# Four small products moved apart on TensorE, and one unit of the inverse transform placed a quad earlier

## The chip, the core and the metric

The program runs on one core of a Trainium2 chip. The time is the device time of that core in microseconds, as a median of several executions. The engines that work side by side are TensorE (PE in the profile, with PEld for its weight loads), VectorE (DVE), ScalarE (ACT), GpSimd (POOL) and the queues that start DMA transfers (SP). A `L407` in a profile line is a line of the kernel's source, in the numbering of the kernel before the change.

## What is computed

A filter in the frequency domain along the sequence, and then a two-layer network with an ELU between the layers:

```python
batch, seq, dim = (8, 3008, 256)
X = np.fft.rfft(x, axis=1)
F = (filt_r + 1j * filt_i)[None, :, :]
y = np.fft.irfft(X * F, n=x.shape[1], axis=1)
# 24064 tokens of 256, hidden width 2048
h = y.reshape(B * S, D) @ w_in
g = np.where(h > 0.0, h, alpha * (np.exp(np.minimum(h, 0.0)) - 1.0))
out = g @ w_out
```

## The kernel before

The transform of length 3008 = 47 x 64 is done as products with small tables. For each batch there is a first factor forward (`a_unit`), a second one with the filter behind it (`b_unit`, eight units `g` of four frequencies `k2` each), the step back through the second factor (`bi_unit`, which takes two units `g` at a time and is called the double step back), and the third factor (`n_unit`, six units `m`), whose output is the input of the network. The network does the two large products by a scheme of seven products in place of eight, so each of its inputs comes with sums and differences of its four blocks (`combine`).

One *item* of the network is a batch, a part `m` of six, and a quarter `q` of the hidden width. An item is called a *quad*, and a batch has 24 of them. While the network works on batch `b - 1`, the transform of batch `b` is put between its steps, by a plan that says in which quad (numbered 0 to 23 within a batch below), and whether in the middle (`place` 0) or at the end (`place` 1), a unit stands.

The double step back, with 16 products of 24 rows and 32 columns, each on its own 32 x 32 piece of the TensorE array. `a` chooses the piece's rows and the PSUM bank, `p` its columns. In the first one of a batch (`g == 0`) the frequency `k2 = 0` needs a table of its own (`v = 1`) for half of the columns when `a = 0`; so there these four products are split in two halves (`js`), and the count is 20:

```python
    def bi_unit(b, g):
        z = ss.pop((b, g))
        t = t3s[b, g] = t3p.tile([P, 2, 4, D], FP32, tag="t3", name="t3")
        pv = [bank("pv") for _ in range(4)]
        for p in range(4):
            for a, (_, ps) in enumerate(pv):
                for js, v in ((slice(0, 1), 1), (slice(1, 2), 0)) if g == a == 0 else ((slice(0, 2), 0),):
                    r = slice(32 * a, 32 * a + 24)
                    nc.tensor.matmul(ps[32 * p:32 * p + 32, js, :], bb[r, v, p, :], z[r, p, js, :],
                                     start=True, stop=True, tile_position=(32 * a, 32 * p))      # L407
        for a, (i, ps) in enumerate(pv):
            nc.scalar.activation(out=t[:, :, a, :], in_=ps, func=AXT.Copy)                       # L410
            banks.append(i)
```

`bank()` hands out four PSUM banks in turn; a matmul into a bank waits until its last reader is done. The third factor, and the sums:

```python
    def n_unit(b, m):
        t, w, h = t4s.pop((b, m)), tns.pop((b, m)), half(m)
        rows = []
        for dh in range(2):
            y = yp.tile([P, 512], FP32, tag="y%d" % dh, name="y%d" % dh)
            k, ps = bank("psn", (P, 512))
            for q, i in enumerate(order(m)):
                nc.tensor.matmul(ps[:, ts(q, P)], ...)                                          # L441
            nc.scalar.activation(out=y[:, 0:2 * h], in_=ps[:, 0:2 * h], func=AXT.Copy)          # L443
            banks.append(k)
            rows += [y[:, 0:h], y[:, h:2 * h]]
        s = yp.tile([P, 3, 256], FP32, tag="ys", name="ys")
        ys[b, m] = combine(*rows, *(s[:, i, 0:h] for i in range(3)))

    def combine(b11, b12, b21, b22, t1, t2, t4):
        nc.vector.tensor_tensor(out=t1, in0=b12, in1=b11, op=ALU.subtract)      # L464
        nc.vector.tensor_tensor(out=b12, in0=b22, in1=b12, op=ALU.subtract)     # L465
        nc.vector.tensor_tensor(out=t2, in0=b22, in1=t1, op=ALU.subtract)       # L466
        nc.vector.tensor_tensor(out=t4, in0=b21, in1=t2, op=ALU.subtract)       # L467
        ...
```

The steps of an item up to the hidden layer (`U`), cut to what the text speaks of. Step `s4` adds onto the bank that step `s7` filled, so its matmul (phd L489) must wait until VectorE has read that bank for `b22` (L497):

```python
        def mm(n, key, start): ...                                   # L489, bank "ph" + key
        def add(o, i0, i1): nc.vector.tensor_tensor(...)             # L497
        def s2(): add("b11", mm(2, "a", True), g["t1"]); done("a")
        ...
        def s7(): add("b22", mm(7, "d", True), g["t4"]); elu_max("b11", g["b11"])
        def s3(): ...
        def s4(): add("b21", mm(4, "d", False), g["t2"]); done("d"); elu_max("b22", g["b22"])
```

The steps down (`D`, L571) multiply with `w_out`; after the last quad of a part, `c_unit` makes four more sums of its result on VectorE (L587). The plan, and the order of the steps in a quad:

```python
                for g in range(NG):
                    s = t + 9 + g + g // 2
                    at(s, 1, b_unit, b, g)          # quads 9 10 12 13 15 16 18 19, at the end
                    ...
                    if g % 2:
                        opens.add(s + 2)
                        at(s + 1, 1, bi_unit, b, g - 1)     # quads 11 14 17 20, at the end
                        at(s + 1, 1, y_write, b, g - 1)
            for m, (s, place) in enumerate(((23, 0), (25, 1), (29, 1), (32, 0), (36, 0), (41, 0))):
                if b > 0 or m > 0:
                    at(t + s - 2, 0, tn_read, b, m)
                    at(t + s - 2, 0, y_read, b, m)
                    at(t + s, place, n_unit, b, m)          # m = 5: quad 41 - 24 = 17, in the middle
                at(t + PER + 4 * m + 5, 0, c_unit, b, m)    # quads 5 9 13 17 21 1, in the middle
                at(t + PER + 4 * m + 6, 0, o_unit, b, m)
        ...
            for k in "DUUDUDDU" if i in opens else "UUDUDDU": ...
            for fn, a in plan.get((i, 0), ()): fn(*a)
            for k in "DUUDUD" if i in opens else "DUUDUDD": ...
            if up_tail: up_tail()
            if down_tail: down_tail()
            for fn, a in plan.get((i, 1), ()): fn(*a)
```

Of the kernel before, what the change touches and what calls it, by code (L numbers as in the profile page):

```python
# [122 lines left out]
def order(m):  # L123

    return (1, 2, 3, 0) if m == 0 else tuple(range(4 * m, 4 * m + 4))
# [3 lines left out]
def kernel(  # L129
# [9 lines left out]
    nc = tc.nc  # L139
# [6 lines left out]
    def pool(name, bufs, **kw):  # L146
        return ctx.enter_context(tc.tile_pool(name=name, bufs=bufs, **kw))
# [21 lines left out]
    bb = pairs[:, P:3 * P].rearrange("p (v a i) -> p v a i", v=2, a=4)  # L169
# [8 lines left out]
    xs, tas, tns, t1s, t2s, ss, t3s, t4s, zs, yds, ys, g_of, po_of, cs_, sds = ({} for _ in range(15))  # L178
# [8 lines left out]
    def bank(name, shape=(P, 2, D)):  # L187
        i = banks.pop(0)
        return i, psM.tile(list(shape), FP32, tag="m%d" % i, name=name)
# [209 lines left out]
    def bi_unit(b, g):  # L399
        z = ss.pop((b, g))  # L400
        t = t3s[b, g] = t3p.tile([P, 2, 4, D], FP32, tag="t3", name="t3")
        pv = [bank("pv") for _ in range(4)]
        for p in range(4):
            for a, (_, ps) in enumerate(pv):
                for js, v in ((slice(0, 1), 1), (slice(1, 2), 0)) if g == a == 0 else ((slice(0, 2), 0),):
                    r = slice(32 * a, 32 * a + 24)
                    nc.tensor.matmul(ps[32 * p:32 * p + 32, js, :], bb[r, v, p, :], z[r, p, js, :],  # L407
                                     start=True, stop=True, tile_position=(32 * a, 32 * p))
        for a, (i, ps) in enumerate(pv):
            nc.scalar.activation(out=t[:, :, a, :], in_=ps, func=AXT.Copy)  # L410
            banks.append(i)
# [18 lines left out]
    def half(m):  # L430

        return 224 if m == 0 else 256
# [8 lines that stand above are left out]
                nc.tensor.matmul(ps[:, ts(q, P)], t[:, i - 4 * m, ds(dh * P, P)], w[:, i - 4 * m, :],  # L441
                                 start=True, stop=True)
            nc.scalar.activation(out=y[:, 0:2 * h], in_=ps[:, 0:2 * h], func=AXT.Copy)  # L443
            banks.append(k)
            rows += [y[:, 0:h], y[:, h:2 * h]]
        s = yp.tile([P, 3, 256], FP32, tag="ys", name="ys")
        ys[b, m] = combine(*rows, *(s[:, i, 0:h] for i in range(3)))

# [11 lines left out]
# [6 lines that stand above are left out]
        return {1: b11, 2: b21, 3: b22, 4: t4, 5: t1, 6: t2, 7: b12}  # L468
# [207 lines left out]
    def w_join(k):  # L676
        q, j = divmod(k, 4)
        m, e, f, l = wts.pop(k)
        hi = wds.pop(k)[:, :, 1]
        nc.vector.scalar_tensor_tensor(out=e, in0=hi, scalar=0x80000000, in1=e,  # L680
                                       op0=ALU.bitwise_and, op1=ALU.bitwise_or)
        nc.vector.tensor_tensor(out=f, in0=f, in1=l, op=ALU.add)
        e = e.bitcast(FP32)
        if j < 2:
            f, e = (t.rearrange("p (a j c) -> p a j c", a=2, j=2) for t in (f, e))
            dst = w_in[q][:, 2 * j:2 * j + 2, :, :].rearrange("p j a c -> p a j c")
            nc.vector.tensor_tensor(out=dst, in0=f, in1=e, op=ALU.mult)
        else:

            f, e = (t.rearrange("p (i a e s) -> p i e a s", i=2, a=4, e=2) for t in (f, e))  # L690
            dst = w_out[q][:, 0:4, j - 2, :].rearrange("p (i e) (a s) -> p i e a s", i=2, a=4)
            for i in range(2):
                nc.vector.tensor_tensor(out=dst[:, i], in0=f[:, i], in1=e[:, i], op=ALU.mult)
        if j % 2 == 1 and k < 15:
            w_sums(k)

    def w_sums(k):
        q, j = divmod(k, 4)
        w = (w_in if j < 2 else w_out)[q]
        a11, a21, a12, a22, s1, s2, s4 = (w[:, i] for i in range(7))  # L700
        nc.vector.tensor_tensor(out=s1, in0=a21, in1=a22, op=ALU.add)
        nc.vector.tensor_tensor(out=s2, in0=s1, in1=a11, op=ALU.subtract)
        nc.vector.tensor_tensor(out=s4, in0=a12, in1=s2, op=ALU.subtract)
        nc.vector.tensor_tensor(out=a21, in0=a11, in1=a21, op=ALU.subtract)
# [30 lines left out]
    with tc.manual_schedule():  # L735
# [108 lines left out]
        ep = pool("ep", 2)  # L844
        op = pool("op", 1)
        n_unit(0, 0)
        w_join(14)


# [4 lines left out]
        def at(quad, place, fn, *a):  # L854
            plan.setdefault((quad, place), []).append((fn, a))
# [13 lines left out]
        for b in range(B):  # L869
            t = (b - 1) * PER  # L870
            if b > 0:
                for c, s in enumerate((2, 2, 4, 4, 7, 7)):
                    at(t + s, 0, x_unit, b, c)
                    if c % 2 == 0:
                        opens.add(t + s + 1)
                        at(t + s, 1, a_unit, b, c)
                    nb, nxt = (b, c + XBUFS) if c + XBUFS < NXC else (b + 1, c + XBUFS - NXC)
                    if nb < B:
                        at(t + s, 1, x_load, nb, nxt)
                    at(t + s, 1, z_write, b, c)  # L880
                for g in range(NG):
                    s = t + 9 + g + g // 2
                    at(s, 1, b_unit, b, g)
                    at(s - 2, 1, f_read, b, g)
                    at(s - 2, 1, z_read, b, g)
                    if g % 2:

                        opens.add(s + 2)
                        at(s + 1, 1, bi_unit, b, g - 1)
                        at(s + 1, 1, y_write, b, g - 1)  # L890
            for m, (s, place) in enumerate(((23, 0), (25, 1), (29, 1), (32, 0), (36, 0), (41, 0))):
                if b > 0 or m > 0:
                    at(t + s - 2, 0, tn_read, b, m)
                    at(t + s - 2, 0, y_read, b, m)
                    at(t + s, place, n_unit, b, m)
                at(t + PER + 4 * m + 5, 0, c_unit, b, m)
                at(t + PER + 4 * m + 6, 0, o_unit, b, m)

        items = [(b, m, q) for b in range(B) for m in range(6) for q in range(4)]
        for i in range(-PER, len(items) + 3):  # L900
# [3 lines left out]
            for k in "DUUDUDDU" if i in opens else "UUDUDDU":  # L904
                s = ups if k == "U" else downs
# [4 lines left out]
            for k in "DUUDUD" if i in opens else "DUUDUDD":  # L910
                s = ups if k == "U" else downs
# [40 lines left out]
```

## Time and profile before

| | |
|---|---|
| time, median of 3 executions | 2637.86 us (2635.85 to 2638.11) |
| the execution that was profiled | 2634.84 us, span 2632.7 us |
| PE busy (matmuls) | 2580.3 us, 98% |
| PEld busy (weight loads) | 2220.9 us, 84% |
| DVE busy | 1861.9 us, 71% |
| ACT busy | 1505.4 us, 57% |
| POOL busy | 488.8 us, 19% |
| mean granted TensorE clock | 0.995 |

The span starts with about 100 us for the first batch's transform and the weights; after that the network runs in a pattern of some 318.5 us for each batch until the end. A float32 matmul stands as two records in the trace. A busy share of 98% for PE does not say that the array streams data for 98% of the time: [...]records of different 32 x 32 pieces lie over each other.

### The profile page before, as it was taken

What the parts mean: (1) busy time and instruction counts of PE and PEld (TensorE: products, weight loads), DVE (VectorE), ACT (ScalarE), POOL (GpSimd) and SP (SyncE); (2) the same over time, 40 slices, a digit from 0 to 9 for tenths busy, and PEclk for the clock granted to TensorE, in tenths of its full rate; (3) what the DMA queues carried; (4) which work ended last, traced back from release to release, by engine and by line L of the source; (5) the groups of instructions that cost most, each with busy time, mean ns of one, the idle gap of its engine ahead of it and who ended that gap; (6) DMA issues with size and microseconds to landing.
All of it is one profiled execution on the core that took longest, in us unless ns stands there. A gap on an engine that the chain in (4) does not pass through costs nothing.

```text
span 2632.7 us, 41233 instructions
## 1 busy us (share of the span) xinstructions
PE 2580.3 (98%) x15300; PEld 2220.9 (84%) x15300; DVE 1861.9 (71%) x3203; ACT 1505.4 (57%) x2622; POOL 488.8 (19%) x669
## 2 busy tenths in 40 slices
PE   6799999999999999999999999999999999999998
PEld 4688889887898888988889888898889888898887
DVE  6876776677666776777667767677676668766666
ACT  7665555555565555555555555555555555555554
POOL 5102320024100331004300133002330023200000
PEclk9899999999999999999999999999999999999999
DMA  9544222432224232333314331143321332210010
GB/s 296 166 119 101 63 64 56 120 77 70 67 59 115 63 92 48 82 89 81 77 45 104 83 95 47 45 110 95 86 57 43 87 85 63 63 41 20 21 28 16
DMA packets 228840, 206.51 MB, mean 78 GB/s; under 512 B 130962, under 2 KB 194674, under 8 KB 228640
## 3 DMA queue, kind: packets, MB, share of 16 engines
q1 hardware_dynamic: 211328, 166.90, 25.7%
q0 software_dynamic: 15856, 36.25, 4.9%
q8 instruction: 121, 1.98, 0.3%
q10 hardware_dynamic: 1456, 0.72, 0.1%
q14 instruction: 79, 0.65, 0.1%
HBM read 131.91 MB, written 78.17 MB: 80 GB/s over the span
## 4 chain that ended last, share of the span: by engine, by line
PE 95%; DVE 1%; ACT 1%; DMA 0%; issue 0%; DVEq 0%; SPq 0%; ACTq 0%
PE po L571 43%; PE phs L489 25%; PE phd L489 12%; PE pha L489 6%; PE psn L441 3%; PE psr L376 2%; PE psa L228 2%; PE pv L407 1%; DVE ys L464 0%; PE po L324 0%; DMA yd<-t 0%; DVE ys L466 0%; PE psi L376 0%; ACT e L507 0%; DVE g L497 0%
## 5 line engine op out<-in xcount | busy, mean ns | idle before, releaser
L571 PE MATMUL po<-g,wo 128*128 128x256 f32 (+1 forms) x5376 | 1305.4, 376 | 0.0
L571 PEld LDWEIGHTS po<-g,wo 128*128 128x128 f32 x5376 | 1014.4, 190 | 143.8 <-issue 23.0
L500 ACT ACTIVATE g<-phs 128x512 f32<-128x512 f32 (+1 forms) x576 | 339.2, 589 | 823.1 <-PE phs L489 823.1
L497 DVE TENSOR_TENSOR g<-phd,g 128x512 f32<-128x512 f32 (+1 forms) x384 | 259.4, 676 | 402.5 <-ACT e L507 345.5
L507 ACT ACTIVATE e<-e 128x512 f32<-128x512 f32 (+1 forms) x768 | 477.3, 621 | 24.4
L511 DVE SCALAR_TENSOR_TENSOR g<-e,g 128x512 f32<-128x512 f32 (+1 forms) x576 | 397.2, 690 | 1.6 <-ACT e L507 1.3
L489 PE MATMUL phs<-y,wi 128*128 128x256 f32 (+1 forms) x1536 | 394.2, 379 | 0.0
L489 PE MATMUL phs<-ys,wi 128*128 128x256 f32 (+1 forms) x1536 | 387.7, 375 | 1.5 <-ACT g L500 1.5
L506 ACT ACTIVATE e<-g 128x512 f32<-128x512 f32 (+1 forms) x576 | 353.2, 613 | 42.8 <-DVE g L497 25.5
L489 PEld LDWEIGHTS phs<-y,wi 128*128 128x128 f32 x1536 | 284.4, 190 | 55.5 <-issue 11.5
L489 PEld LDWEIGHTS phs<-ys,wi 128*128 128x128 f32 x1536 | 291.4, 190 | 35.4 <-ACT g L500 2.5
L385 POOL TENSOR_TENSOR sr<-sr,zs 128x512 f32<-128x512 f32 x56 | 71.2, 1271 | 1144.5 <-DVE zs L330 1144.5
L511 DVE SCALAR_TENSOR_TENSOR g<-e,phs 128x512 f32<-128x512 f32 (+1 forms) x192 | 129.8, 676 | 126.6 <-ACT e L507 126.6
L489 PE MATMUL phd<-ys,wi 128*128 128x256 f32 (+1 forms) x768 | 195.2, 377 | 7.0 <-DVE g L497 7.0
L506 ACT ACTIVATE e<-phs 128x512 f32<-128x512 f32 (+1 forms) x192 | 113.0, 589 | 148.8 <-PE phs L489 148.7
L489 PE MATMUL phd<-y,wi 128*128 128x256 f32 (+1 forms) x768 | 193.7, 375 | 0.0
L489 PE MATMUL pha<-y,wi 128*128 128x256 f32 (+1 forms) x768 | 193.7, 375 | 0.0
L489 PEld LDWEIGHTS phd<-ys,wi 128*128 128x128 f32 x768 | 144.6, 190 | 28.6 <-DVE g L497 12.8
L497 DVE TENSOR_TENSOR g<-pha,g 128x512 f32<-128x512 f32 (+1 forms) x192 | 129.1, 672 | 53.3 <-PE pha L489 53.0
L489 PEld LDWEIGHTS pha<-y,wi 128*128 128x128 f32 x768 | 145.8, 190 | 16.5
L489 PEld LDWEIGHTS phd<-y,wi 128*128 128x128 f32 x768 | 145.8, 190 | 16.5
L548 DVE TENSOR_TENSOR g<-g,g 128x512 f32<-128x512 f32 (+1 forms) x192 | 130.7, 681 | 6.7
(129 smaller groups left out, 2382.5 us busy)
## 6 DMA issues: line engine op xcount, KB each, us to landing
yd<-t SPq DMA_DIRECT2D x127, 192.0 KB
t<-yd SPq DMA_DIRECT2D x190, 128.0 KB
z<-t SPq DMA_DIRECT2D x84, 256.0 KB
f<-fp POOLq DMA_DIRECT2D x224, 96.0 KB, 3.1
t<-z SPq DMA_DIRECT2D x224, 96.0 KB
out_dram<-o SPq DMA_DIRECT2D x632, 32.0 KB
tn<-tn_t SPq DMA_DIRECT2D x48, 256.0 KB
xc<-in_x_dram SPq DMA_DIRECT2D x84, 128.0 KB
```

What stands on the lines that cost most here:

```text
L228: nc.tensor.matmul(p[o:o + 64, u, :], w[r, u, o:o + 64], src[r, u, :], start=True, stop=True)
L376: nc.tensor.matmul(ps[32 * a:32 * a + 32, c, :], fb[k, 1 if g == a == 0 else 0, c, :], t[k, a, :], start=True, stop=True)
L385: nc.gpsimd.tensor_tensor(out=sr, in0=sr, in1=p, op=ALU.add)
L441: nc.tensor.matmul(ps[:, ts(q, P)], t[:, i - 4 * m, ds(dh * P, P)], w[:, i - 4 * m, :], start=True, stop=True)
L489: nc.tensor.matmul(ps[:, a, 0:h], w_in[q][:, COMBO[n], a, :], y[n], start=start and a == 0, stop=True, skip_group_check=True)
L497: nc.vector.tensor_tensor(out=g[o], in0=i0, in1=i1, op=ALU.add)
L500: nc.scalar.activation(out=g[o], in_=i0, func=AXT.Copy)
L506: nc.scalar.activation(out=e, in_=src, func=AXT.Relu, scale=-1.0)
L507: nc.scalar.activation(out=e, in_=e, func=AXT.Exp, scale=-1.0)
L511: nc.vector.scalar_tensor_tensor(out=g[n], in0=es[n], scalar=1.0, in1=src, op0=ALU.subtract, op1=ALU.max)
L548: nc.vector.tensor_tensor(out=b12, in0=b22, in1=b12, op=ALU.subtract)
L571: nc.tensor.matmul(po[i][:, u, 0:h], w_out[q][:, COMBO[n], a, :], g[n][:, a, :], start=q == 0 and a == 0 and n in (1, 3, 6, 4), stop=True, ...
```

## The change

There are two changes that have nothing to do with each other.

In the first double step back of a batch, the order of the 20 products is another: first the four with the table for `k2 = 0`, then the twelve whole ones of `a = 1, 2, 3`, then the four remaining halves of `a = 0`. Before, the two halves on one piece of the array stood next to each other. The products, their tables and their results are the same; for `g > 0` nothing changes.

The third factor's last unit (`m = 5`) goes from the middle of quad 17 to the middle of quad 16, and its reads from quad 15 to quad 14; its four sums on VectorE are put into a function of their own, which stands at the end of quad 17, behind the double step back of that quad. For all other `m` the sums stay where they were. The aim is to keep the four sums out of the middle of quad 17, where VectorE has products of `b_unit` and the four sums of `c_unit` as well.

```diff
-        for p in range(4):
-            for a, (_, ps) in enumerate(pv):
-                for js, v in ((slice(0, 1), 1), (slice(1, 2), 0)) if g == a == 0 else ((slice(0, 2), 0),):
-                    r = slice(32 * a, 32 * a + 24)
-                    nc.tensor.matmul(ps[32 * p:32 * p + 32, js, :], bb[r, v, p, :], z[r, p, js, :],
-                                     start=True, stop=True, tile_position=(32 * a, 32 * p))
+
+        both = [(p, a, slice(1 if g == a == 0 else 0, 2), 0) for p in range(4) for a in range(4)]
+        if g == 0:
+            both = [(p, 0, slice(0, 1), 1) for p in range(4)] + [w for w in both if w[1]] + [w for w in both if not w[1]]
+        for p, a, js, v in both:
+            r = slice(32 * a, 32 * a + 24)
+            nc.tensor.matmul(pv[a][1][32 * p:32 * p + 32, js, :], bb[r, v, p, :], z[r, p, js, :],
+                             start=True, stop=True, tile_position=(32 * a, 32 * p))
 ...
-        ys[b, m] = combine(*rows, *(s[:, i, 0:h] for i in range(3)))
+        ys[b, m] = rows + [s[:, i, 0:h] for i in range(3)]
+
+    def n_sums(b, m):
+        ys[b, m] = combine(*ys[b, m])
 ...
         n_unit(0, 0)
+        n_sums(0, 0)
 ...
-            for m, (s, place) in enumerate(((23, 0), (25, 1), (29, 1), (32, 0), (36, 0), (41, 0))):
+            for m, (s, place) in enumerate(((23, 0), (25, 1), (29, 1), (32, 0), (36, 0), (40, 0))):
                 if b > 0 or m > 0:
                     at(t + s - 2, 0, tn_read, b, m)
                     at(t + s - 2, 0, y_read, b, m)
                     at(t + s, place, n_unit, b, m)
+
+                    at(*((t + s + 1, 1) if m == 5 else (t + s, place)), n_sums, b, m)
```

## The prediction

> **What bounds the kernel now.** I read the page's busy shares and its chain of work first, then the waits of TensorE, then the two places that the change touches.
>
> ```profile
> PE 2580.3 (98%) x15300; PEld 2220.9 (84%) x15300; DVE 1861.9 (71%) x3203; ACT 1505.4 (57%) x2622; POOL 488.8 (19%) x669
> ...
> PE 95%; DVE 1%; ACT 1%; DMA 0%; issue 0%; DVEq 0%; SPq 0%; ACTq 0%
> ```
>
> TensorE is busy nearly always, and the chain that ended last lies on it for 95%. So time is won only where TensorE waits, or where its instructions run badly, and what is won there shortens the whole kernel as long as no other engine takes over; VectorE at 71% and ScalarE at 57% leave room on average. The waits of TensorE between 200 us and 2600 us, that is in the repeating pattern, are a single row (in total, times, longest):
>
> ```profile
> PE phd L489 <- DVE g L497: 7.0, 7, 1.0
> ```
>
> Seven times a matmul of step `s4` waits for VectorE. One of them is at 969 us, in quad 17 of a batch. The timeline there, first TensorE, then VectorE (start, duration, engine, line, what, idle before it):
>
> ```profile
> 967.15 1.03 PE L571 MATMUL po<-g,wo 128*128 128x256 f32 x4
> 969.17 1.13 PE L489 MATMUL phd<-ys,wi 128*128 128x256 f32 x4 [0.99 <-DVE g L497]
> ...
> 964.30 0.61 DVE L587 TENSOR_TENSOR c<-k,k 128x256 f32<-128x256 f32 x1
> 965.27 1.05 DVE L464 TENSOR_TENSOR ys<-y 128x256 f32<-128x256 f32 x1 [0.36 <-ACT y L443]
> 966.43 0.76 DVE L465 TENSOR_TENSOR y<-y,y 128x256 f32<-128x256 f32 x1
> 967.11 0.94 DVE L466 TENSOR_TENSOR ys<-y,ys 128x256 f32<-128x256 f32 x1
> 968.09 0.43 DVE L467 TENSOR_TENSOR ys<-y,ys 128x256 f32<-128x256 f32 x1
> 968.43 0.68 DVE L497 TENSOR_TENSOR g<-phd,g 128x512 f32<-128x512 f32 x1
> ```
>
> The reader is to see that the add L497, for which the matmul waits, stands directly behind the four sums of the third factor, and these behind a sum of `c_unit`. A group of four matmul records runs on from one start to the next in 0.86 us where nothing holds it (939.62 to 940.48 us in quad 15); here it is 969.17 - 967.15 = 2.02 us, so the loss is 1.16 us: 0.99 us of idle time[...]. All seven lie between 1.15 and 1.17 us. For quad 13, which has products of `b_unit` and a `c_unit` but no third factor, the same place reads:
>
> ```profile
> 911.81 1.03 PE L571 MATMUL po<-g,wo 128*128 128x256 f32 x4
> 912.83 1.13 PE L489 MATMUL phd<-ys,wi 128*128 128x256 f32 x4
> ```
>
> 1.02 us, so 0.16 us is lost there. Then the double step back, in the first one of a batch (g = 0, 40 records) and in the next one (g = 2, 32 records), each with the TensorE instruction that follows it:
>
> ```profile
> 248.86 2.14 PE L407 MATMUL pv<-zs,pairs 24*32 24x256 f32 x40
> 250.93 0.92 PE L571 MATMUL po<-g,wo 128*128 128x256 f32 x3
> ...
> 291.88 1.14 PE L407 MATMUL pv<-zs,pairs 24*32 24x512 f32 x32
> 292.95 0.92 PE L571 MATMUL po<-g,wo 128*128 128x256 f32 x3
> ```
>
> From its start to the next instruction the first takes 2.07 us, the other 1.07 us, though both stream the same number of columns. Why, is seen in the groups of matmuls in flight from 248.85 to 248.99 us, then from 248.99 to 249.25 us, and for g = 2 from 291.85 to 291.99 us:
>
> ```profile
> L407 PE MATMUL pv<-zs,pairs 24*32 24x512 f32 x9 | 0.7, 612 | 0.0
> L407 PE MATMUL pv<-zs,pairs 24*32 24x256 f32 x4 | 0.5, 398 | 0.0
> ...
> L407 PE MATMUL pv<-zs,pairs 24*32 24x256 f32 x8 | 0.7, 386 | 0.0
> L407 PE MATMUL pv<-zs,pairs 24*32 24x512 f32 x9 | 0.7, 612 | 0.0
> ...
> L407 PE MATMUL pv<-zs,pairs 24*32 24x512 f32 x16 | 0.7, 612 | 0.0
> ```
>
> Nine of the twelve whole products start within 0.14 us, and the four first halves; then no further whole one for over 0.25 us. The missing three are the last in program order (p = 3). With g = 2 all sixteen start at once.
>
> [...]nine whole products started while second halves before them in the order still waited. [...]the sums L464 to L467 take 0.42 us at the median and 1.05, 0.76 and 0.94 us in quad 17, where GpSimd adds at the same time; the fourth, after it was done, took 0.43 us.
>
> **The change part by part. First, the order of the products.** It removes no instruction: 20 products, 40 loads and 40 matmul records, seven times in the run (batches 1 to 7). Before, the second half on a piece follows the first in the order[...]. In the new order the four first halves and the twelve whole products [...]start at once, as in g = 2. [...]Their chain on one piece, from the single records of before, is: first pass at 0, second pass 0.24 us later, then the other half's passes 0.22 us apart, at 0.46 and 0.67 us, and 0.37 us for the last one's record: 1.05 us, and 0.04 us more for the fourth piece, 1.09 us. The whole products need 1.14 us, as in g = 2. So the halves lie beside them, and I put the start of the next instruction at 1.10 us, 0.03 us above g = 2 for the later issue. Gain 2.07 - 1.10 = 0.97 us, times 7: 6.8 us. Behind it ScalarE empties the bank of a = 0 first, which is now filled last, at about 1.09 us; in g = 2 it is also filled near the end, and the copies began there 1.3 us after the start of the products. So I expect the copies at the same distance and no new wait beyond the 0.1 us that g = 2 shows.
>
> **Second, the sums.** Without the third factor in its middle, quad 17 becomes what quad 13 is now: products, c sums, then L497. The four sums with their gaps hold VectorE from 965.27 to 968.43 us, 3.16 us; TensorE loses 1.16 us of that, and should lose 0.16 us as in quad 13. Gain 1.00 us, times 7: 7.0 us. The eighth batch's last unit has no transform beside it and no wait now, so nothing is won there.
>
> Third, what is added elsewhere. The 16 matmul records of the third factor (1.78 us) move from quad 17 to quad 16, nothing gained or lost. In quad 16 ScalarE gets its two copies (1.07 us) before the two copies L576 (1.07 us): before, it was through with L507 at 951.45 us and its next need, the copy for L506, was at 952.31 us; with both pairs it ends about 953.6 us, and TensorE, itself 1.75 us later there, asks at about 954.05 us. No wait. At the end of quad 17 VectorE gets four sums of 0.42 us, 1.7 us; it idled 0.99 us there before L497 reads pha (976.01 us), so that add comes about 0.7 us later. What needs it is ScalarE's L506 some 4 us later and a bank that comes round later still. No wait.
>
> Sum: 6.8 + 7.0 = 13.8 us, and 2637.86 - 13.8 = 2624.1 us. Nothing else on TensorE changes.
>
> **The rivals.** (1) The order gives little: the four first halves now stand on the same rows of the array, and if products of one row group can't run together, they cost 4 x 0.43 us (two records of 0.22 us each) one after the other before the rest. [...]Against it: g = 2 puts four products on each row group and ends in 1.14 us. Only the sums would count: 2631 us. (2) The wait of ScalarE's copies takes over: bank a = 0 is filled last and copied first, so step `s1` of the next quad waits for it. Were the copies 0.5 us later than I think, 3.5 us of the gain would go: 2628 us. (3) The sums only move the wait: in quad 18 VectorE has L497, the transposes of `o_unit` and then new products; or ScalarE in quad 16 comes late. For it: 0.99 us of idle time does not hold 1.7 us. Against it: the slack of several us above. It would leave 2627 to 2631 us. (4) [...]the second halves still delay the next instruction by 0.2 us: 2625.5 us.
>
> **Range and chances.** The two parts are independent, both read from measured neighbours (g = 2, quad 13). I take 2624.5 us, a little above the sum for small waits. Both parts failing by half gives 2631; both a little better than thought (0.16 us gone too) gives 2622. Range 2620.5 to 2630. Even the whole gain is 0.5%, so faster by over 2% has 0.005, slower by over 2% 0.005, within 2% the rest.
>
> **What would show it.** In the profile after: the first double step back with 12 whole products and four halves in flight within the first 0.15 us, and about 1.10 us to the next instruction; the row of waits phd on L497 gone, or no single wait above 0.1 us; sums L464 to L467 in quad 17 behind L551 at about 0.42 us each; L443 of m = 5 in quad 16. Wrong it would be if a row of waits of some 0.5 us or more, seven times, appeared on phs for L410, or on phd in quads 16 or 18, or if the first double step back stayed above 1.5 us.

## The result, and the profile after

| | time, median | ratio to before, 95% interval |
|---|---|---|
| before | 2637.99 us | |
| after, the first measurement | 2619.72 us | 0.9933 (0.9916 to 0.995) |
| after, measured again on another occasion (`again_after`) | 2622.15 us | 0.9944 (0.993 to 0.9958) |

The first measurement gives 18.3 us, more than the 13.4 us of the prediction, and its time lies 0.8 us below the predicted range. The second, of the same kernel, gives 0.56% of 2637.99 us, 14.8 us, with an interval from 11.1 to 18.5 us. On that occasion one execution of the kernel before took 8303 us and one of the kernel after 12739 us; both are left out of the figures here.

The page of the kernel after, busy shares and chain of work:

```profile
PE 2569.9 (98%) x15300; PEld 2220.2 (85%) x15300; DVE 1852.8 (71%) x3203; ACT 1504.0 (57%) x2622; POOL 486.9 (19%) x669
...
PE 96%; DMA 0%; DVE 0%; ACT 0%; issue 0%; DVEq 0%; SPq 0%; ACTq 0%
```

The work is the same to the instruction, and TensorE still sets the end; its busy time fell by 10.4 us. Of that 7 x (2.14 - 1.29) = 6.0 us is the double step back, whose products lie closer over each other, and 2.7 us falls ahead of the first matmul of the network (63.10 us busy before, 60.38 us after), which the change does not touch. TensorE's waits from 200 us to 2600 us are an empty list: the row of phd is gone. Quad 17 of the same batch as before, TensorE and VectorE (phd is now L494, its read L502, the c sums L592, the four sums L469 to L472):

```profile
962.86 1.03 PE L576 MATMUL po<-g,wo 128*128 128x256 f32 x4
963.73 1.03 PE L494 MATMUL phd<-ys,wi 128*128 128x256 f32 x4
964.59 0.38 PE L576 MATMUL po<-g,wo 128*128 128x256 f32 x1
...
961.75 0.61 DVE L592 TENSOR_TENSOR c<-k,k 128x256 f32<-128x256 f32 x1
962.29 0.68 DVE L502 TENSOR_TENSOR g<-phd,g 128x512 f32<-128x512 f32 x1
...
969.42 0.42 DVE L469 TENSOR_TENSOR ys<-y 128x256 f32<-128x256 f32 x1
969.87 0.42 DVE L470 TENSOR_TENSOR y<-y,y 128x256 f32<-128x256 f32 x1
970.21 0.42 DVE L471 TENSOR_TENSOR ys<-y,ys 128x256 f32<-128x256 f32 x1
970.67 0.42 DVE L472 TENSOR_TENSOR ys<-y,ys 128x256 f32<-128x256 f32 x1
```

The read L502 stands behind the c sums at once, and phd follows the group before it after 0.87 us, where undisturbed groups stand 0.86 us apart. The four sums now take 0.42 us each, when GpSimd has no sum of its own under way (its last one ended at 965.32 us). Then the first double step back, with the instruction that follows it:

```profile
249.66 1.29 PE L409 MATMUL pv<-zs,pairs 24*32 24x256 f32 x40
250.88 0.92 PE L576 MATMUL po<-g,wo 128*128 128x256 f32 x3
```

and the groups of matmuls in flight in its first 0.14 us (249.65 to 249.79 us):

```profile
L409 PE MATMUL pv<-zs,pairs 24*32 24x512 f32 x12 | 0.7, 612 | 0.0
L409 PE MATMUL pv<-zs,pairs 24*32 24x256 f32 x4 | 0.4, 398 | 0.0
```

All twelve whole products and the four first halves start at once, and the next instruction comes after 1.22 us instead of 2.07 us. One period, from a batch's first double step back to the next batch's, is 316.40 us in place of 318.51 us, in every one of six periods within 0.03 us.

### The profile page after: what moved, and what is told of

Same layout as the page of the kernel before. It is cut to its first block, busy times and chain, and to the rows that moved or that the text cites. A ratio compares the mean times of both kernels' runs of the same rounds, so it can differ in the third digit from the quotient of the medians.

```text
span 2618.7 us, 41226 instructions
## 1 busy us (share of the span) xinstructions
PE 2569.9 (98%) x15300; PEld 2220.2 (85%) x15300; DVE 1852.8 (71%) x3203; ACT 1504.0 (57%) x2622; POOL 486.9 (19%) x669
## 4 chain that ended last, share of the span: by engine, by line
PE 96%; DMA 0%; DVE 0%; ACT 0%; issue 0%; DVEq 0%; SPq 0%; ACTq 0%
PE po L576 44%; PE phs L494 25%; PE phd L494 12%; PE pha L494 6%; PE psn L443 3%; PE psr L376 2%; PE psa L228 2%; PE pv L409 1%; PE po L324 0%; DMA yd<-t 0%; PE psi L376 0%; DMA t<-yd 0%; PE psr L324 0%; DVE c L592 0%; PE psi L324 0%
## 5 line engine op out<-in xcount | busy, mean ns | idle before, releaser
L576 PE MATMUL po<-g,wo 128*128 128x256 f32 (+1 forms) x5376 | 1306.1, 376 | 0.0
L576 PEld LDWEIGHTS po<-g,wo 128*128 128x128 f32 x5376 | 1016.2, 190 | 139.1 <-issue 20.0
L502 DVE TENSOR_TENSOR g<-phd,g 128x512 f32<-128x512 f32 (+1 forms) x384 | 259.4, 675 | 413.3 <-ACT e L512 322.2
L494 PE MATMUL phs<-y,wi 128*128 128x256 f32 (+1 forms) x1536 | 394.5, 380 | 0.0
L494 PE MATMUL phs<-ys,wi 128*128 128x256 f32 (+1 forms) x1536 | 387.9, 375 | 1.5 <-ACT g L505 1.5
L494 PEld LDWEIGHTS phs<-y,wi 128*128 128x128 f32 x1536 | 284.9, 191 | 55.1 <-issue 11.5
L494 PEld LDWEIGHTS phs<-ys,wi 128*128 128x128 f32 x1536 | 291.9, 190 | 34.9 <-ACT g L505 2.5
L494 PE MATMUL phd<-ys,wi 128*128 128x256 f32 (+1 forms) x768 | 194.6, 376 | 0.0
L494 PE MATMUL phd<-y,wi 128*128 128x256 f32 (+1 forms) x768 | 193.8, 375 | 0.0
L494 PE MATMUL pha<-y,wi 128*128 128x256 f32 (+1 forms) x768 | 193.8, 375 | 0.0
L494 PEld LDWEIGHTS phd<-ys,wi 128*128 128x128 f32 x768 | 145.4, 190 | 19.0 <-DVE g L502 3.0
L494 PEld LDWEIGHTS pha<-y,wi 128*128 128x128 f32 x768 | 146.1, 190 | 16.3
L494 PEld LDWEIGHTS phd<-y,wi 128*128 128x128 f32 x768 | 146.1, 190 | 16.2
L502 DVE TENSOR_TENSOR g<-pha,g 128x512 f32<-128x512 f32 (+1 forms) x192 | 129.2, 673 | 40.5 <-PE pha L494 40.2
```

What stands on the lines that cost most here:

```text
L494: nc.tensor.matmul(ps[:, a, 0:h], w_in[q][:, COMBO[n], a, :], y[n], start=start and a == 0, stop=True, skip_group_check=True)
L502: nc.vector.tensor_tensor(out=g[o], in0=i0, in1=i1, op=ALU.add)
L576: nc.tensor.matmul(po[i][:, u, 0:h], w_out[q][:, COMBO[n], a, :], g[n][:, a, :], start=q == 0 and a == 0 and n in (1, 3, 6, 4), stop=True, ...
```

## The experiments

Periods are means over six periods of one trace. The last column is the difference of medians to the kernel before that ran beside it.

| run | period, us | first double step back to next instruction, us | ratio to before (95%) | difference, us |
|---|---|---|---|---|
| `again_before` | 318.50 | 2.07 | 1.0001 (0.9993 to 1.001) | +0.6 |
| `again_after` | 316.40 | 1.22 | 0.9944 (0.993 to 0.9958) | -13.5 |
| `order_alone` | 317.67 | 1.22 | 0.9975 (0.9966 to 0.9985) | -5.5 |
| `sums_alone` | 317.24 | 2.07 | 0.9967 (0.9954 to 0.998) | -8.0 |
| `halves_first` | 316.87 | 1.70 | 0.9949 (0.9936 to 0.9961) | -14.2 |
| `q16_sums_with` | 317.04 | 1.22 | 0.9959 (0.9947 to 0.9972) | -12.1 |
| `q17_sums_end` | 316.40 | 1.22 | 0.9946 (0.9934 to 0.9959) | -14.9 |
| `c_split` | 316.14 | 1.22 | 0.9939 (0.9926 to 0.9953) | -16.7 |
| `quad12_plain` | 316.92 | 2.00 | 0.9958 (0.9941 to 0.9974) | -11.9 |

Medians are uncertain by one to two microseconds, so effects of 2 us are read from the period, which repeats to 0.03 us, and not from the time.

**Both kernels again.** No edit.

> The kernel before, unchanged, against itself. Both theories: ratio 1.000, and its interval tells how far the median of a few executions can be off. Theory A (the gain is what the trace's two places show, 7 x (0.85 + 1.27) = 14.8 us, and the measured 18.3 us has some 3.5 us of luck in it): single executions spread over about 4 us, and the profiled span can differ by a microsecond or more in the first 250 us with the same period of 318.5 us. Theory B (3.5 us more are really won somewhere): executions agree within about 1 us.

> The changed kernel, unchanged, once more. Theory A: ratio about 0.9944 (14.8 us below the kernel before), period of 316.40 us in the trace. Theory B: ratio 0.9931 again (18.3 us).

The kernel before comes out at 1.0001 against itself, the kernel after at 0.9944, the ratio that the two places in the trace give; the interval alone would allow 11.1 to 18.5 us. The single executions of the kernel before went from 2633.24 to 2638.04 us on that occasion. The traces tell more closely. From the first double step back to the end of the span it is 2383.86 and 2383.82 us in the two traces of the kernel before, 2369.08 and 2369.06 us in the two of the kernel after: 14.8 us less each time. What differs between traces of one kernel lies ahead of that. The first matmul of the network starts at 100.79 us in the trace of `again_before`, and at 97.11 us in that of `halves_first`, which up to there is the same program but ran on another chip. That is 3.7 us of difference ahead of everything that the change touches. On one and the same chip the four traces of `again_before`, `again_after`, `order_alone` and `sums_alone` have this matmul between 98.25 and 100.79 us. Theory A holds: of the 18.3 us of the first measurement, 3.5 us are luck. On the second occasion the median was 2.4 us lower for the kernel before and 2.4 us higher for the kernel after. What makes the start vary is open.

**Each part alone.** `order_alone` is the kernel before with the new order of products, `sums_alone` the kernel after with the old order:

```diff
 # order_alone, against before: the loop of bi_unit as in the change, nothing else
 # sums_alone, against after:
-        if g == 0:
-            both = [(p, 0, slice(0, 1), 1) for p in range(4)] + ...
-        for p, a, js, v in both: ...
+        for p in range(4):
+            for a, (_, ps) in enumerate(pv): ...      # the old loop
```

> Only the order of the products in the first double step back; the third factor stays in quad 17 with its sums. Theory A (two independent gains): the first double step back takes 1.22 us to the next instruction instead of 2.07 us, period 318.52 - 0.85 = 317.67 us, time 5.9 us below before, ratio 0.9977; the wait of phd on VectorE (7 times 0.99 us) is still there. Rival (the gains depend on each other, the time won in quad 11 is given back in quad 17): period 318.5 us, ratio 1.000.

> Only the move of the third factor's last unit and of its sums; the order of the products is that of before. Theory A: no wait of phd on VectorE is left, the first double step back still takes 2.07 us, period 318.52 - 1.27 = 317.25 us, time 8.9 us below before, ratio 0.9966. With order_alone the two add up to 14.8 us. Rival (part of the gain needs both): the two do not add up, by over 2 us.

Periods of 317.67 and 317.24 us against 318.51 us: 0.84 us and 1.27 us, and 0.84 + 1.27 = 2.11 us is what both together save. They are independent. In `order_alone` the wait is there in full (in total, times, longest):

```profile
PE phd L490 <- DVE g L498: 7.0, 7, 1.0
```

**How many products start at once.** In the kernel before, nine whole products and four first halves start within 0.15 us. Three second halves, which start only at 0.46, 0.49 and 0.52 us, stand between them in the order: together these are the first 16 products. `halves_first` puts the second halves before the whole products, and by the same count eight whole ones should start at once:

```diff
-            both = [(p, 0, slice(0, 1), 1) for p in range(4)] + [w for w in both if w[1]] + [w for w in both if not w[1]]
+            both = [(p, 0, slice(0, 1), 1) for p in range(4)] + [w for w in both if not w[1]] + [w for w in both if w[1]]
```

> The changed kernel with another order in the first double step back: four first halves, then the four second halves, then the twelve whole products. Theory W[...]: four first halves and exactly 8 whole products start within 0.15 us; the ninth to twelfth enter[...] at about 0.65 us, and end at about 1.69 us, so 1.6 us to the next instruction instead of 1.22 us; 2.7 us slower than the changed kernel. Rival H (a second half waiting for its piece stops all that stands behind it): no whole product starts before about 0.24 us. Rival N (only halves that stand next to each other cost): all twelve start at once, and 1.2 us to the next instruction.

The matmuls in flight from 247.01 to 247.16 us, 0.14 us after its start:

```profile
L409 PE MATMUL pv<-zs,pairs 24*32 24x512 f32 x8 | 0.7, 612 | 0.0
L409 PE MATMUL pv<-zs,pairs 24*32 24x256 f32 x4 | 0.4, 398 | 0.0
```

Exactly eight whole products. With the 4 first and the 4 second halves that stand before them in the order they make 16 products. Rival H would have none here, rival N twelve. Of the other four, the single records show the first at 0.43 us, just after the first of the two records of the very first product had ended (0.40 us), and the rest at 0.65, 0.69 and 0.74 us, when its second record had ended too (0.61 us). In the kernel before, the tenth whole product starts at 0.86 us, when the first record of the first second half has ended (0.83 us). That the ends of these records let the later products start is my reading of the times; no run shows it. The next instruction came after 1.70 us; expected was 1.6 us, since I had all four at 0.65 us. The period is 0.47 us longer than after's.

**Where the sums may stand.**

```diff
 # q16_sums_with: the sums with their unit, in the middle of quad 16
-                    at(*((t + s + 1, 1) if m == 5 else (t + s, place)), n_sums, b, m)
+                    at(t + s, place, n_sums, b, m)
 # q17_sums_end: the unit stays in the middle of quad 17 (41, 0), its sums at the end of quad 17
+                    at(*((t + s, 1) if m == 5 else (t + s, place)), n_sums, b, m)
```

> The changed kernel, but the four sums stand with their unit in the middle of quad 16 instead of at the end of quad 17. Theory D (what matters is that VectorE reads phd in time, and the sums must not stand before that read): in quad 16 the sums begin at about the end of the two copies and push the read of phd by about 1 us; the matmul of step s4 has 0.7 us of slack there, so 0.2 to 0.6 us are lost, seven times: 1.5 to 4 us slower than the changed kernel. Rival (quad 17 alone was full; in quad 16 there is room as there are no c sums): same as the changed kernel within 0.5 us, no wait in quad 16.

> The third factor's unit stays in the middle of quad 17 as before, only its four sums go to the end of quad 17; the products are in the new order. Theory D (the sums before the read of phd are the whole cause): no wait of phd is left in quad 17, time as the changed kernel within 0.5 us, period 316.4 us. Rival (the matmuls of the unit had to leave quad 17 as well): some of the 1.27 us comes back, up to 8.9 us.

With the sums in quad 16 the wait came back, smaller, in the form that quad 17 had before (VectorE, then TensorE):

```profile
631.33 0.44 DVE L469 TENSOR_TENSOR ys<-y 128x256 f32<-128x256 f32 x1 [2.73 <-ACT y L445]
631.87 0.77 DVE L470 TENSOR_TENSOR y<-y,y 128x256 f32<-128x256 f32 x1
632.56 0.94 DVE L471 TENSOR_TENSOR ys<-y,ys 128x256 f32<-128x256 f32 x1
633.53 0.42 DVE L472 TENSOR_TENSOR ys<-y,ys 128x256 f32<-128x256 f32 x1
633.88 0.68 DVE L502 TENSOR_TENSOR g<-phd,g 128x512 f32<-128x512 f32 x1
...
634.61 1.13 PE L494 MATMUL phd<-ys,wi 128*128 128x256 f32 x4 [0.38 <-DVE g L502]
```

VectorE had been idle for 2.73 us before the sums and the wait came all the same: they can't begin before ScalarE's copies, and that is just ahead of the read of phd. The period is 0.64 us longer than after's. `q17_sums_end` has after's period to 0.01 us and no wait. So it was not needed to move the unit to quad 16; to take the four sums away from the read of phd is the whole effect of the second change. The rival that the matmuls had to leave quad 17 as well falls.

Not told apart is GpSimd's share. In quad 17 of the kernel before, its own sums run beside the four:

```profile
966.12 0.79 POOL L389 TENSOR_TENSOR zs<-si 128x256 f32<-128x256 f32 x1
966.87 0.90 POOL L390 TENSOR_TENSOR zs<-si 128x256 f32<-128x256 f32 x1
```

There the four sums hold VectorE for 3.16 us, in quad 16 above, where GpSimd's last two sums run from 631.56 to 633.22 us, for 633.88 - 631.33 = 2.55 us, and at the end of quad 17, without GpSimd's, for 971.01 - 969.42 = 1.59 us. An estimate from these figures: at the pace of 1.59 us the read of phd would come 1.57 us and 0.96 us earlier, more than the 0.99 us and 0.38 us that TensorE sat idle, so neither wait would have arisen with the sums where they stood. No run moved GpSimd's sums alone.

**Why quad 13 still loses 0.27 us and quad 17 nothing.** Two runs. `c_split` defers two of the c sums in quad 13, `quad12_plain` gives quad 12 the plain order of steps. (A quad in `opens`, called opened, begins with a step down; 12, 15, 18 and 21 are.)

```diff
 # c_split
-            rest = [(p7, p7, c12), (c12, c12, p35), (c21, po[3][:, 0, 0:h], p7), (c22, p7, p5)]
-            cs_[b, m] = c, lambda: [add(*r) for r in rest]
+            rest = [(p7, p7, c12), (c21, po[3][:, 0, 0:h], p7), (c12, c12, p35), (c22, p7, p5)]
+            cs_[b, m] = c, lambda lo=0, hi=4: [add(*r) for r in rest[lo:hi]]
...
-                at(t + PER + 4 * m + 5, 0, c_unit, b, m)
+                for k in range(2) if m == 2 else (None,):
+                    at(t + PER + 4 * m + 5, k or 0, c_unit, b, m, *(() if k is None else (2 * k, 2 * k + 2)))
 # quad12_plain
-                        opens.add(s + 2)
+                        if g != 1:
+                            opens.add(s + 2)
```

> The changed kernel, and in quad 13 two of the four c sums go to the end of the quad, behind the double step's neighbours, so that VectorE reads phd about 1.2 us earlier. Theory D: the 0.16 us before phd and the 0.1 us in its group in quad 13 go, 0.27 us seven times: period 316.13 us, 1.9 us faster than the changed kernel. Rival (that delay is a weight load which stays, whatever VectorE does): period 316.40 us.

> The changed kernel, but quad 12 does not begin with a step down: its steps stand in the plain order, as in quad 16. What is to be told apart is why quad 13 loses 0.27 us before phd and quad 17, now with the same load on VectorE, loses nothing. Theory O (the order of the quad before: in an opened quad the last step up stands one group of four records, 0.86 us, nearer to its end, so VectorE comes 0.86 us later into the next quad): with quad 12 plain VectorE reads phd in quad 13 about 0.86 us earlier against TensorE, and the loss of 0.27 us there is gone; at the start of quad 12, on the other hand, step s1 comes 0.86 us earlier and waits for ScalarE's copies, some 0.7 to 0.9 us; in all 3 to 5 us slower than the changed kernel, period 316.8 to 317.1 us. Rival P (what differs is the work in quad 12 or 13 itself): the loss of 0.27 us in quad 13 stays.

The kernel after in quad 13, TensorE and VectorE:

```profile
907.51 1.03 PE L576 MATMUL po<-g,wo 128*128 128x256 f32 x4
908.54 1.13 PE L494 MATMUL phd<-ys,wi 128*128 128x256 f32 x4
909.50 0.81 PE L576 MATMUL po<-g,wo 128*128 128x256 f32 x3
...
907.80 0.68 DVE L502 TENSOR_TENSOR g<-phd,g 128x512 f32<-128x512 f32 x1
```

The read starts 0.29 us after the group L576 that stands before phd; in quad 17 (above) it starts 962.86 - 962.29 = 0.57 us ahead of that group. That is 0.86 us, one group. In `quad12_plain` quad 13 reads

```profile
591.83 1.03 PE L576 MATMUL po<-g,wo 128*128 128x256 f32 x4
592.70 1.03 PE L494 MATMUL phd<-ys,wi 128*128 128x256 f32 x4
593.56 1.89 PE L576 MATMUL po<-g,wo 128*128 128x256 f32 x8
...
591.25 0.68 DVE L502 TENSOR_TENSOR g<-phd,g 128x512 f32<-128x512 f32 x1
```

with the read 0.58 us ahead and no loss: theory O holds. The price is at the start of quad 12, where `s1` now stands directly behind the double step back and waits for ScalarE's copies out of it:

```profile
PE phs L494 <- ACT t L412: 5.0, 7, 0.7
```

Hence the next instruction comes after 2.00 us in place of 1.22 us; less the 0.26 us won in quad 13, that is the period of 316.92 us, 0.52 us longer than after's. In `c_split` the loss in quad 13 is gone too,

```profile
589.36 1.03 PE L576 MATMUL po<-g,wo 128*128 128x256 f32 x4
590.22 1.03 PE L494 MATMUL phd<-ys,wi 128*128 128x256 f32 x4
```

and its period is 316.14 us, the expected 0.26 us less, 1.8 us in seven batches. It is the best version by its period; the intervals of its ratio (0.9926 to 0.9953) and of after's overlap, so the times alone don't show it.

## Why the prediction was right and where it was wrong

Three steps failed: the step "should lose 0.16 us as in quad 13", where TensorE loses nothing (1.27 us won each time in place of 1.00 us); the start of the next instruction behind the first double step back at 1.10 us, which is 1.22 us; and the range, which left too little room for the spread of executions. The first two miss in opposite directions, by +1.9 us and -0.8 us in seven batches, so it is partly luck that their sum is off by 1.0 us alone.

- That TensorE bounds the kernel, and that what is won on it passes to the end: right. Seven periods shortened by 2.11 us make 14.8 us, and the second measurement has 0.9944.
- The order of products: right in kind: the four halves and the twelve whole products, the first 16 of the order, start within 0.10 us of each other. The term "the start of the next instruction at 1.10 us" was too small; it measured 1.22 us, so the gain is 0.85 us and not 0.97 us each. I put the four second halves at 0.46 us and just after, as they follow the first halves on their own pieces in the kernel before. The records show the first of them at 0.46 us and the other three at 0.65 to 0.68 us, when the second record of the first product had ended (0.61 us); the late whole products of `halves_first` come in the same two steps (0.43 us, then 0.65 us and later). What held the three back was not shown. So the last record of the halves ends at 1.29 us in place of 1.09 us.
- The copies: right. They start 251.01 - 249.66 = 1.35 us after the products, where I expected 1.3 us, and no new wait came.
- The sums: the mechanism was right, the term was mis-sized: 1.00 us in the prediction, 1.27 us measured. Two errors. I measured the loss between the starts of two groups (1.16 us) and overlooked that the waiting group itself runs 0.1 us longer (969.17 to 970.14 us before is 0.97 us, not 0.86 us). And the step "quad 17 becomes what quad 13 is now" was wrong: quad 13 follows an opened quad and quad 17 doesn't, so it keeps nothing of the loss; `quad12_plain` shows it.
- The rivals: (1) and (3) fell, (4) had the right kind of delay, 0.15 us above g = 2. Rival (2), a wait for the copies, didn't come in the change, but it did in `quad12_plain`, so it was a real one. That VectorE or ScalarE would be late in quads 16 and 18 didn't happen.
- The sum: 7 x (0.85 + 1.27) = 14.8 us against 13.8 us in the working and 13.4 us in the stated time. The rest of the 18.3 us is the spread of executions. The range's lower end was set from the two gains: the case "0.16 us gone too" was put at 2622 us (its sum is 2637.86 - 13.8 - 7 x 0.16 = 2622.9 us), and 1.5 us were left below it. With both terms right the time would be 2637.99 - 14.8 = 2623.2 us, inside the range; the 3.5 us of spread carried the time out.

## What to carry to other kernels

An engine in the background that is idle for nearly a third of the time (VectorE, busy for 71%) can still make the bounding engine wait, here seven times for 0.99 us: what counts is which instruction stands directly before the one that is needed soon, so put work without a near deadline behind the last urgent read, as the four sums show. With small products packed on the array, count products: in the three orders measured here no product behind the first 16 started at once, so one that has to wait for its predecessor on the same piece should stand behind 16 which can start. And when effects of a few microseconds are predicted for a program of milliseconds, read them from a period inside the trace, and put the spread of single executions into the range.

## What the runs showed of the hardware

- Of the 20 products of the first double step back, those which started in the first 0.15 us all stood among the first 16 of the program order, in all three orders: 9, 12 and 8 whole products, with the halves ahead of them in the order just those that make 16. Matmuls of different 32 x 32 pieces started out of program order (in the kernel before whole products at 0.01 to 0.09 us, second halves ahead of them in the order at 0.46 to 0.52 us). On one piece, the second half started 0.46 us after the first half, on all four pieces of the kernel before.
- A matmul that waited 0.99 us for VectorE cost TensorE 1.27 us. Of the rest, 0.17 us lies ahead of its group: undisturbed groups are 1.03 us long and start 0.86 us apart, so each starts 0.17 us before the one ahead of it ends. And 0.10 us lies within it: its second record followed the first after 0.32 us, in an undisturbed group after 0.22 us. Its first weight load started with the group (969.17 us); in an undisturbed group it started 0.22 us ahead (940.26 and 940.48 us).
- The start of the program, about 100 us of loads and of the first batch's transform, varied by 3.7 us between traces with the same instructions, while the 318.5 us periods behind it repeated to 0.03 us.
